# Two chained MLPs behind a chunked scan on one core: other places for the sums and remainders of the next block pair, and PSUM pools split in two

## The chip, the cores and the metric

One core of a Trainium2 chip runs the whole program in one launch. The metric is device time in microseconds (us); lower is better. The engines that matter here are TensorE (PE, matrix products), VectorE (DVE), ScalarE (ACT), GpSimd (POOL) and SyncE (SP, which issues most transfers).

## The reference

Three stages follow each other, all in float32.

```python
# 1. scan over x (4, 8, 768, 32) in chunks of 32: y = intra-chunk part + inter-chunk state part
# 2. first MLP on 3072 tokens of 256 features (d_ff 2048)
h = x @ w_in
g = np.where(h > 0.0, h, np.exp(np.minimum(h, 0.0)) - 1.0)
x = g @ w_out
# 3. second, gated MLP (d_ff 1536)
g = x @ w_gate
silu = g * (1.0 / (1.0 + np.exp(-g)))
val = x @ w_val
return (silu * val @ w_out).astype(np.float32)
```

## The kernel before, in words

**Layout.** The 3072 tokens are six blocks of 512 (`BLOCKS`). Features lie on the partitions, so a block is two tiles of 128x512, `x2[b][:, 0]` and `x2[b][:, 1]`. A float32 product is made of three TensorE products on a high part and a remainder: high x high, low x high, high x low (`mm3`, L548). The high part is a copy into the type float32r on ACT, the remainder a subtraction on DVE or POOL.

**Opening.** The scan runs in 24 units of 128 tokens. The first four units (block 0) are written out by hand in `ORDER` (L57). Odd units put their products into the PSUM tiles `cb_odd` and `y_odd` (named cbo and yo in the profile), two banks each, both of the pool `ps0` (L106). After the last entry of `ORDER`, L836 gives this pool back, and L837 opens the pool `ps` in its place, with two buffers of the tag `h` and one each of `c0` and `c1`. The last readers of `cb_odd` are L443 (DVE), those of `y_odd` L541 and L477 (DVE).

**First MLP.** Its 96 steps (6 blocks x 16 slices of 128 hidden features) are the loop at L941. Step i makes the hidden tile (`m_a`: six matmuls into `h`), then ACT and DVE apply the activation (`m_e1`, `m_e1b`; L578, L583, L584), the tile is split (`m_e2`; L561 on ACT, L562 on POOL), and the output product of three steps earlier follows (`m_c`, L605). Two buffers of `h` mean that step i+2 can't begin before DVE's L584 of step i is done. The scan units of later blocks, the weights' decoding and the preparation of the second MLP are tasks in the tables `early`, `mid`, `pe` and `late`, keyed by step. `last_a` is step 79; steps 80 to 95 are the last block.

**Second MLP.** Two blocks together are a pair p (three pairs); for each of the twelve slices f of the hidden features there is a step `s_step(j)` with j = 12p + f. The gate and value columns of a slice and the two blocks of a pair form a 2x2 product, made with seven products instead of eight. For that, each pair needs seven operands (`OPS`, L56): the four tiles b11, b21, b12/t1 and b22 and the sums t3, t1, t2, t4 (`x_sum`, L684), each with a high part (`x_hi`, L704 on ACT) and a remainder (`x_lo`, L708). They are kept in tiles `xs`; pair 1 has tiles of its own (suffix "o" in the profile) for b11, t2 and t3, and all other operands of pairs 1 and 2 overwrite those of pair 0.

A step issues on PE: 12 matmuls for the products a, b, d and c, nine more for a (b21), d (t4) and c (b22), then the 12 output matmuls `s_o` of the step before (named o, L556). Between them lie on DVE: u2 (L762, from b), u3 (L763, from d), u3 again (L770), s1 (L777), u2 again (L778), m0 (L779) and m1 (L784). On ACT: the copy of a (L758), the split of the second hidden tile of the step before (L749), the copy of c (L764), two Silu (L775, L781) and the split of the first hidden tile (L749). On POOL: the two remainders of these splits (gl, L750). The product d with t4 writes on top of what L763 has just read, so it waits for L763.

Everything else in a step is called at hooks: "a" (behind L764 in program order, ahead of L770), "b" (behind the Silu of L775, ahead of L777), "c" (behind the first split) and "d" (at the end of the step). Each engine works its instructions off in program order. The table `hooks` is filled at L904 to L920: weights of later slices (`w2_load`, `w2_hi`, `w2_sums` on POOL, `w2_lo` on DVE, all of pair 0's steps 0 to 9), and the operands of the next pair. For pair p with e = 12p the four sums are on POOL at hook "c" of steps e-5 to e-2; the high parts are at hooks "b" and "c" of steps e-3 to e-1, and their remainders on DVE at hook "d" of the same steps (t4 on POOL; b22 at hook "a" of step e).

**End of a pair.** In the second step of the next pair, `s_end` (L720) copies the four output tiles from PSUM (m = 0 on DVE, m = 1 on ACT) and issues their transfers; the last pair does so at its end (L792), where the first hidden tile's remainder is on POOL and the second's on DVE.

Of the kernel before, what the change touches and what calls it, by code (L numbers as in the profile page):

```python
# [8 lines left out]
F32 = mybir.dt.float32  # L9
F32R = mybir.dt.float32r  # L10
# [3 lines left out]
AF = mybir.ActivationFunctionType  # L14
ALU = mybir.AluOpType
PSUM = bass.MemoryType.PSUM
# [12 lines left out]
NF1, NF2 = F1 // 128, F2 // 128  # L29
# [3 lines left out]
LAG = 3  # L33
# [22 lines left out]
OPS = ["b11", "t2", "t3", "t1", "b21", "t4", "b22"]  # L56
# [10 lines left out]
def ssm_mlp_glu_kernel(ctx, tc, a, bcs, xbc, w1, w2, consts, out):  # L67
    nc = tc.nc
    NB = len(BLOCKS)
# [4 lines left out]
    work = ctx.enter_context(tc.tile_pool(name="work", bufs=3))  # L74
# [6 lines left out]
    x2 = [x2_all[:, 2 * s:2 * (s + n)].rearrange("p (k q) -> p k q", k=2) for s, n in zip(starts, BLOCKS)]  # L81
# [13 lines left out]
    ph2 = {}  # L95
# [7 lines left out]
    cb_ps = psa.tile([128, 2, 512], F32, name="cb")  # L103
    y_ps = psa.tile([128, 2, 512], F32, name="y")
    first = ExitStack()
    ps0 = first.enter_context(tc.tile_pool(name="ps0", bufs=1, space=PSUM))  # L106
    cb_odd = ps0.tile([128, 2, 512], F32, name="cbo")
    y_odd = ps0.tile([128, 2, 512], F32, name="yo")
    ap_ = ats.enter_context(tc.tile_pool(name="attn", bufs=2))
    ast = ats.enter_context(tc.tile_pool(name="attn_static", bufs=1))  # L110
    sbd = [ast.tile([128, 2, 128], F32, name=f"sbd{i}") for i in range(2)]
# [436 lines left out]
    def mm3(dst, pairs, first, last, **kw):  # L548

        ops = []  # L550
        for (lh, ll), (rh, rl) in pairs:
            ops += [(lh, rh), (ll, rh)]
        for (lh, ll), (rh, rl) in pairs:
            ops.append((lh, rl))
        for i, (l, r) in enumerate(ops):
            nc.tensor.matmul(dst, lhsT=l, rhs=r, start=first and i == 0, stop=last and i == len(ops) - 1, **kw)  # L556
# [7 lines left out]

    def m_a(b, f):
        n = BLOCKS[b]
        h = hps[b, f] = ph2["ps"].tile([128, 512], F32, tag="h", name="h", bufs=2)[:, :n]
        wh, wl = W1["i", f]
        mm3(h, [((wh[:, k], wl[:, k]), (xh_t[b][:, k], xl_t[b][:, k])) for k in range(2)], True, True)

# [19 lines left out]
    def m_c(b, f):  # L590
        n = BLOCKS[b]
        if f == 0:
            cps[b] = [ph2["ps"].tile([128, 512], F32, tag=f"c{m}", name=f"c{m}")[:, :n] for m in range(2)]
        g = gt.pop((b, f))
        if b == 0:
            for m in range(2):
                nc.tensor.matmul(cps[b][m], lhsT=W1["v", f][:, m * 128:(m + 1) * 128], rhs=g, start=f == 0, stop=f == NF1 - 1)  # L597
            return
        wh, wl = W1["o", f]
        gh, gl = g  # L600
        prods = [(m, w, r) for r, ws in ((gh, (wh, wl)), (gl, (wh,))) for m in range(2) for w in ws]
        if f in (0, NF1 - 1):
            prods.sort(key=lambda z: z[0])
        for m, w, r in prods:
            nc.tensor.matmul(cps[b][m], lhsT=w[:, m * 128:(m + 1) * 128], rhs=r,  # L605
                             start=f == 0 and w is wh and r is gh, stop=f == NF1 - 1 and r is gl)
# [84 lines left out]
    def x_hi(p, nm):  # L691
        if (p, nm) not in xs:
            k = OPS.index(nm)
            if p == 1 and k < 3:
                if k < 2:
                    z = ph2["w2l" if k else "w2h"].tile([128, WS], F32R, tag="v2", name=f"x_{nm}o")
                else:
                    z = ph2["w2h"].tile([128, 1024], F32R, name=f"x_{nm}o")
                xs[p, nm] = z[:, :512], z[:, 512:1024]
            elif p == 0:  # L700
                xs[p, nm] = [ph2["xs"].tile([128, 512], F32R, name=f"x_{nm}{z}") for z in "hl"]
            else:
                xs[p, nm] = xs[0, nm]
        nc.scalar.activation(xs[p, nm][0], XT[p][nm], AF.Copy)  # L704
# [5 lines left out]
    def s_half(j, i):  # L710
        return (ident8.rearrange("p h q -> p (h q)"))[:, 512 * i:512 * i + 512]

    def s_o(j, i, m):
        p, f = divmod(j, NF2)
        if f == 0:
            ops_[p, i, m] = ph2["ps"].tile([128, 512], F32, tag="h" if i else f"c{m}", name=f"o{i}{m}", bufs=2 if i else None)
        ms = slice(384 + m * 128, 384 + m * 128 + 128)
        mm3(ops_[p, i, m], [([w[:, ms] for w in W2[f]], gt[j, i])], f == 0, f == NF2 - 1)

    def s_end(p, i, m):  # L720
        b = 2 * p + i
        y = x2[b - 1][:, m] if i else ph2["w2h"].tile([128, 512], F32, tag="yo", name="yo", bufs=2)
        if m == 0:
            nc.vector.tensor_copy(y, ops_.pop((p, i, m)))
        else:
            nc.scalar.activation(y, ops_.pop((p, i, m)), AF.Copy)
        nc.sync.dma_start(out[m * 128:(m + 1) * 128, starts[b]:starts[b] + 512], y)

    def s_step(j, hooks):
        p, f = divmod(j, NF2)  # L730

        def hook(nm):
            for fn, args in hooks.get((j, nm), []):
                fn(*args)

        ps = {k: ph2["psv"].tile([128, 512], F32, tag=f"p{k}", name=f"p{k}") for k in "abcd"}

        def prod(k, w, nm, first):
            ws = slice(128 * w, 128 * w + 128)
            (wh, wl), (xh, xl) = [z[:, ws] for z in W2[f]], xs[p, nm]  # L740
            for i, (l, r) in enumerate(((wh, xh), (wl, xh), (wh, xl))):
                nc.tensor.matmul(ps[k], lhsT=l, rhs=r, start=first and i == 0, stop=i == 2, skip_group_check=True)  # L742

        def mtile(nm):
            return work.tile([128, 512], F32, tag="m", name=nm)

        def g_split(j, i, m, eng):
            hi, lo = [work.tile([128, 512], F32R, tag=f"g{z}", name=f"g{z}", bufs=LAG + 1) for z in "hl"]
            nc.scalar.activation(hi, m, AF.Copy)  # L749
            eng.tensor_tensor(lo, m, hi.bitcast(F32), ALU.subtract)  # L750
            gt[j, i] = hi, lo

        prod("a", 0, "b11", True)
        prod("b", 7, "t2", True)
        prod("d", 5, "t3", True)
        prod("c", 6, "t1", True)
        s1 = mtile("s1")
        nc.scalar.activation(s1, ps["a"], AF.Copy)  # L758
        if j:
            g_split(j - 1, 1, V.pop(j - 1), nc.gpsimd)  # L760
        u2, u3, s5 = s_half(j, 0), s_half(j, 1), x2[2 * max(p - 1, 0) + 1][:, 1]
        nc.vector.tensor_tensor(u2, s1, ps["b"], ALU.add)  # L762
        nc.vector.tensor_tensor(u3, u2, ps["d"], ALU.add)  # L763
        nc.scalar.activation(s5, ps["c"], AF.Copy)  # L764
        hook("a")
        if f == 1 and p:
            for i in range(2):
                for m in range(2):
                    s_end(p - 1, i, m)
        nc.vector.tensor_tensor(u3, u3, s5, ALU.add)  # L770
        prod("a", 1, "b21", False)
        prod("d", 2, "t4", False)
        prod("c", 8, "b22", False)
        m0 = mtile("m0")
        nc.scalar.activation(m0, ps["a"], AF.Silu)  # L775
        hook("b")
        nc.vector.tensor_tensor(s1, u2, ps["d"], ALU.add)  # L777
        nc.vector.tensor_tensor(u2, u2, ps["c"], ALU.add)  # L778
        nc.vector.tensor_tensor(m0, m0, s1, ALU.mult)  # L779
        m1 = mtile("m1")  # L780
        nc.scalar.activation(m1, u2, AF.Silu)  # L781
        g_split(j, 0, m0, nc.gpsimd)
        hook("c")
        nc.vector.tensor_tensor(m1, m1, u3, ALU.mult)  # L784
        V[j] = m1
        hook("o")
        if j:
            for i in range(2):
                for m in range(2):
                    s_o(j - 1, i, m)  # L790
                gt.pop((j - 1, i))
        if j == 3 * NF2 - 1:  # L792
            g_split(j, 1, V.pop(j), nc.vector)
            for i in range(2):
                for m in range(2):
                    s_o(j, i, m)
                    s_end(p, i, m)
        hook("d")


# [1 line left out]
    with tc.manual_schedule():  # L802
# [31 lines left out]
        for z in ORDER:  # L834
            tok[z]()
        first.close()  # L836
        ph2["ps"] = ctx.enter_context(tc.tile_pool(name="ps", bufs=1, space=PSUM))  # L837

        early, mid, pe, late = {}, {}, {}, {}
        late[8] = [(lambda: nc.scalar.activation(ident8, ident.unsqueeze(1).to_broadcast([128, H, Q]), AF.Copy), ())]  # L840
# [1 line left out]
        def at(when, slot, fn, *args):  # L842
            when.setdefault(slot, []).append((fn, args))
# [61 lines left out]
        for f in range(NHL, NF2):  # L905
# [4 lines left out]
            at(hooks, (f - 2, "b"), w2_hi, f, 1)  # L910
            at(hooks, (f - 2, "b"), w2_lo, f, 0)
            at(hooks, (f - 2, "d"), w2_lo, f, 1)
        for p in range(1, NB // 2):
            e = p * NF2
            for k, nm in enumerate(("t3", "t1", "t2", "t4")):
                at(hooks, (e - 5 + k, "c"), x_sum, p, nm, nc.gpsimd)
            for k, nm in enumerate(OPS):
                i, h, l = [(e - 3, "b", "d"), (e - 2, "b", "d"), (e - 2, "c", "d"), (e - 1, "b", "d"), (e - 1, "b", "d"), (e - 1, "c", "d"), (e - 1, "c", "a")][k]
                at(hooks, (i, h), x_hi, p, nm)
                at(hooks, (i + (l == "a"), l), x_lo, p, nm, nc.gpsimd if nm == "t4" else nc.vector)  # L920

        seq1 = [(b, f) for b in range(NB) for f in range(NF1)]
        def go(tasks):
# [96 lines left out]
```

## Time and profile before

| what | us |
|---|---|
| median of 3 runs | 621.52 |
| lowest and highest run | 617.13 and 621.55 |
| profiled execution, its own time | 621.05 |
| its span, first to last instruction | 619.3 |
| PE, DVE, ACT, POOL busy in it | 596.2, 468.5, 369.6, 365.0 |

The profiled execution's own time is 1.75 us longer than its span. The opening takes up to 23.9 us, the first MLP from there to 329.4, the second MLP from there to the end. "Busy" counts instructions in flight on an engine; matmuls are pipelined, so that one of 0.39 us starts every 0.23 us.

### The profile page before, as it was taken

How to read it: one execution, taken by the hardware profiler on the slowest of the kernel's cores; microseconds unless marked ns; L12 is line 12 of the kernel's file. 1: busy time of each engine (PE TensorE's matmuls, PEld its weight loads, DVE VectorE, ACT ScalarE, POOL GpSimd, SP SyncE). 2: the span in 40 equal slices, each digit the busy share in tenths (PEclk: the TensorE clock that was granted, in tenths of full speed). 3: DMA queues.
4: the chain of work that ended last, by engine and by line, in shares of the span. 5: the costliest groups of instructions: out<-in, count | busy, mean ns of one | idle time of the engine just before them, and what ended most of it. 6: DMA issues, size and time to landing. Idle time of an engine off the chain costs nothing.

```text
span 619.3 us, 9832 instructions
## 1 busy us (share of the span) xinstructions
PE 596.2 (96%) x3524; PEld 469.7 (76%) x3524; DVE 468.5 (76%) x676; ACT 369.6 (60%) x659; POOL 365.0 (59%) x326
## 2 busy tenths in 40 slices
PE   6899999999999999999999999978999998999997
PEld 4556667888888888778878777866888886888885
DVE  6898866768878789795644999899666679766664
ACT  1456657776668667776876555545544455544443
POOL 4444559997887887774765666756333456333332
PEclk9999999999999999999999999999999999999999
DMA  7698533345466666622010011100100000100001
GB/s 210 214 287 244 180 100 113 111 138 174 164 178 207 203 200 205 212 78 78 25 52 23 29 52 52 52 1 0 69 1 1 1 0 1 69 1 1 1 0 68
DMA packets 22744, 58.70 MB, mean 95 GB/s; under 512 B 3736, under 2 KB 6168, under 8 KB 22696
## 3 DMA queue, kind: packets, MB, share of 16 engines
q1 hardware_dynamic: 20664, 53.18, 27.6%
q10 hardware_dynamic: 2032, 4.90, 2.1%
q8 instruction: 27, 0.44, 0.3%
q14 instruction: 21, 0.17, 0.1%
HBM read 50.12 MB, written 7.96 MB: 94 GB/s over the span
## 4 chain that ended last, share of the span: by engine, by line
PE 62%; issue 10%; DVE 6%; POOL 5%; DMA 4%; ACT 1%; POOLq 0%; DVEq 0%; ACTq 0%
PE h L556 16%; PE c L605 15%; PE o L556 10%; PE pd L742 5%; POOL gl L750 5%; PE pa L742 5%; PE pc L742 4%; DMA w2e<-in_w 4%; PE pb L742 3%; PE cb L432 1%; PE y L509 1%; PE c L597 1%; DVE w2l L670 1%; DVE ident L763 1%; DVE ident L762 1%
## 5 line engine op out<-in xcount | busy, mean ns | idle before, releaser
L750 POOL TENSOR_TENSOR gl<-m,gh 128x512 fp32r<-128x512 f32 x71 | 94.6, 1333 | 133.6 <-ACT gh L749 133.6
L562 POOL TENSOR_TENSOR gl<-m,gh 128x512 fp32r<-128x512 f32 x80 | 110.6, 1383 | 43.5 <-ACT gh L561 42.1
L584 DVE SCALAR_TENSOR_TENSOR m<-m,h 128x512 f32<-128x512 f32 x96 | 65.5, 683 | 55.1 <-ACT m L583 53.2
L578 ACT ACTIVATE m<-h 128x512 f32<-128x512 f32 x96 | 56.8, 592 | 48.4 <-PE h L556 42.4
L556 PE MATMUL h<-xh,wih 128*128 128x512 f32 x192 | 81.3, 424 | 2.9 <-DVE x L477 1.9
L556 PE MATMUL h<-xh,wil 128*128 128x512 f32 x192 | 76.1, 396 | 0.0
L605 PE MATMUL c<-gh,woh 128*128 128x512 f32 x160 | 62.4, 390 | 0.0
L605 PE MATMUL c<-gh,wol 128*128 128x512 f32 x160 | 62.3, 389 | 0.0
L583 ACT ACTIVATE m<-m 128x512 f32<-128x512 f32 x96 | 59.8, 623 | 0.5
L556 PE MATMUL h<-xl,wih 128*128 128x512 f32 x192 | 59.8, 393 | 0.0
L781 ACT ACTIVATE m<-ident 128x512 f32<-128x512 f32 x36 | 22.8, 633 | 61.4 <-DVE ident L778 61.4
L556 PE MATMUL o<-gl,w2h 128*128 128x512 f32 x144 | 56.2, 390 | 0.4 <-POOL gl L750 0.4
L556 PE MATMUL o<-gh,w2h 128*128 128x512 f32 x144 | 56.2, 390 | 0.0
L556 PE MATMUL o<-gh,w2l 128*128 128x512 f32 x144 | 56.1, 390 | 0.0
L762 DVE TENSOR_TENSOR ident<-s,pb 128x512 f32<-128x512 f32 x36 | 24.6, 683 | 40.4 <-PE pb L742 36.6
L561 ACT ACTIVATE gh<-m 128x512 fp32r<-128x512 f32 x80 | 50.1, 626 | 6.0 <-DVE m L584 5.8
L605 PE MATMUL c<-gl,woh 128*128 128x512 f32 x160 | 50.9, 389 | 0.0
L556 PEld LDWEIGHTS h<-xh,wih 128*128 128x128 f32 x192 | 36.6, 190 | 15.4 <-DVE m L584 3.5
L393 POOL TENSOR_TENSOR xb<-xb,P 128x128 f32<-128x128 f32 x16 | 38.0, 2374 | 14.2 <-DVE P L387 14.2
L749 ACT ACTIVATE gh<-m 128x512 fp32r<-128x512 f32 x72 | 45.2, 628 | 1.2 <-DVE m L779 1.0
L764 ACT ACTIVATE x<-pc 128x512 f32<-128x512 f32 x36 | 21.5, 598 | 35.3 <-PE pc L742 35.3
L556 PEld LDWEIGHTS h<-xl,wih 128*128 128x128 f32 x192 | 36.5, 190 | 8.0
(226 smaller groups left out, 1470.9 us busy)
## 6 DMA issues: line engine op xcount, KB each, us to landing
w2e<-in_w SPq DMA_DIRECT2D x12, 768.0 KB
abc<-ac SPq DMA_DIRECT2D x16, 512.0 KB
bcraw<-in_bcs SPq DMA_DIRECT2D x32, 256.0 KB
w2e<-in_w SPq DMA_DIRECT2D x14, 512.0 KB
xb<-in_xbc SPq DMA_DIRECT2D x18, 256.0 KB
v2d<-w2e ACTq DMA_DIRECT2D x12, 384.0 KB
v<-v2d SPq DMA_DIRECT2D x12, 384.0 KB
out_y<-yo SPq DMA_DIRECT2D x6, 256.0 KB
```

The lines of the kernel that those rows point to most:

```text
L393: nc.gpsimd.tensor_tensor(u["ct"], u["ct"], u["P"], ALU.mult)
L556: nc.tensor.matmul(dst, lhsT=l, rhs=r, start=first and i == 0, stop=last and i == len(ops) - 1, **kw)
L561: nc.scalar.activation(hi, src, AF.Copy)
L562: lo_eng.tensor_tensor(lo, src, hi.bitcast(F32), ALU.subtract)
L578: nc.scalar.activation(m, h, AF.Relu, scale=-1.0)
L583: nc.scalar.activation(m, m, AF.Exp, scale=-1.0)
L584: nc.vector.scalar_tensor_tensor(m, m, -1.0, h, ALU.add, ALU.max)
L605: nc.tensor.matmul(cps[b][m], lhsT=w[:, m * 128:(m + 1) * 128], rhs=r, start=f == 0 and w is wh and r is gh, stop=f == NF1 - 1 and r is gl)
L742: nc.tensor.matmul(ps[k], lhsT=l, rhs=r, start=first and i == 0, stop=i == 2, skip_group_check=True)
L749: nc.scalar.activation(hi, m, AF.Copy)
L750: eng.tensor_tensor(lo, m, hi.bitcast(F32), ALU.subtract)
L762: nc.vector.tensor_tensor(u2, s1, ps["b"], ALU.add)
```

## The change

The PSUM tiles `cb_odd` and `y_odd` lie in two pools, and so do the tags `h` and `c0`/`c1` that take their place. The operand t1 of pair 1 has tiles of its own, in the place of the two buffers `yo`; the outputs are copied into `x2` tiles of a later pair instead. The four sums of pair 1 are on DVE in steps 88 to 91 of the first MLP, those of pair 2 on DVE at hook "b" of steps 15 to 18. High parts and remainders are together at one hook: for pair 1, t3 at "d" of step 0, b11 and t2 at "b" of step 10, t1 at "a" of step 11; for pair 2, b11, t2, t3, t1 at "b" of steps 18 to 21; b21 at "b" of step e-1, with the high parts of t4 and b22 behind it, t4's remainder on POOL at "d" of e-1, and b22's on DVE at "a" of step e. At the end of the last step, the first hidden tile's remainder is on DVE, the last output matmuls are in another order, and the last output tile is copied in two halves on DVE and ACT.

```diff
-    ps0 = first.enter_context(tc.tile_pool(name="ps0", bufs=1, space=PSUM))
-    cb_odd = ps0.tile([128, 2, 512], F32, name="cbo")
-    y_odd = ps0.tile([128, 2, 512], F32, name="yo")
+    cb_odd = first.enter_context(tc.tile_pool(name="ps0", bufs=1, space=PSUM)).tile([128, 2, 512], F32, name="cbo")
+    y_odd = first.enter_context(tc.tile_pool(name="ps1", bufs=1, space=PSUM)).tile([128, 2, 512], F32, name="yo")
...
-            if p == 1 and k < 3:
+            if p == 1 and k < 4:
...
-    def s_end(p, i, m):
+    def s_end(p, i, m, cut=False):
         b = 2 * p + i
-        y = x2[b - 1][:, m] if i else ph2["w2h"].tile([128, 512], F32, tag="yo", name="yo", bufs=2)
-        if m == 0:
-            nc.vector.tensor_copy(y, ops_.pop((p, i, m)))
+        y, o = x2[min(2 * p + 2, NB - 2) + i][:, m], ops_.pop((p, i, m))
+        if cut:
+            nc.vector.tensor_copy(y[:, :256], o[:, :256])
+            nc.scalar.activation(y[:, 256:], o[:, 256:], AF.Copy)
+        elif m == 0:
+            nc.vector.tensor_copy(y, o)
...
-        g_split(j, 0, m0, nc.gpsimd)
+        end = j == NB // 2 * NF2 - 1
+        g_split(j, 0, m0, None if end else nc.gpsimd)
...
-        if j == 3 * NF2 - 1:
+        if end:
+            nc.vector.tensor_tensor(gt[j, 0][1], m0, gt[j, 0][0].bitcast(F32), ALU.subtract)
             g_split(j, 1, V.pop(j), nc.vector)
-            for i in range(2):
+            for k in range(2):
                 for m in range(2):
-                    s_o(j, i, m)
-                    s_end(p, i, m)
+                    s_o(j, 0, m, (slice(0, 2), slice(2, 3))[k])
+            for m in range(2):
+                s_end(p, 0, m)
+            for m in range(2):
+                s_o(j, 1, m)
+                s_end(p, 1, m, m)
...
-        ph2["ps"] = ctx.enter_context(tc.tile_pool(name="ps", bufs=1, space=PSUM))
+        ph2["h"] = ctx.enter_context(tc.tile_pool(name="ps", bufs=1, space=PSUM))
+        ph2["c"] = ctx.enter_context(tc.tile_pool(name="psc", bufs=1, space=PSUM))
...
-        for p in range(1, NB // 2):
+        for k, nm in enumerate(("t3", "t1", "t2", "t4")):
+            at(late, last_a + 9 + k, x_sum, 1, nm, nc.vector)
+            at(hooks, (NF2 + 3 + k, "b"), x_sum, 2, nm, nc.vector)
+        for p, where in ((1, dict(t3=(0, "d"), t1=(11, "a"), b11=(10, "b"), t2=(10, "b"))), (2, dict(b11=(18, "b"), t2=(19, "b"), t3=(20, "b"), t1=(21, "b")))):
             e = p * NF2
-            for k, nm in enumerate(("t3", "t1", "t2", "t4")):
-                at(hooks, (e - 5 + k, "c"), x_sum, p, nm, nc.gpsimd)
-            for k, nm in enumerate(OPS):
-                i, h, l = [(e - 3, "b", "d"), (e - 2, "b", "d"), (e - 2, "c", "d"), (e - 1, "b", "d"), (e - 1, "b", "d"), (e - 1, "c", "d"), (e - 1, "c", "a")][k]
-                at(hooks, (i, h), x_hi, p, nm)
-                at(hooks, (i + (l == "a"), l), x_lo, p, nm, nc.gpsimd if nm == "t4" else nc.vector)
+            for nm, z in where.items():
+                at(hooks, z, x_hi, p, nm)
+                at(hooks, z, x_lo, p, nm, nc.vector)
+            at(hooks, (e - 1, "b"), x_hi, p, "b21")
+            at(hooks, (e - 1, "b"), x_lo, p, "b21", nc.vector)
+            at(hooks, (e - 1, "b"), x_hi, p, "t4")
+            at(hooks, (e - 1, "b"), x_hi, p, "b22")
+            at(hooks, (e - 1, "d"), x_lo, p, "t4", nc.gpsimd)
+            at(hooks, (e, "a"), x_lo, p, "b22", nc.vector)
```

## Rows read from the trace of the kernel before

**Rows 1.** The page's busy time by engine, whole span.

```profile
PE 596.2 (96%) x3524; PEld 469.7 (76%) x3524; DVE 468.5 (76%) x676; ACT 369.6 (60%) x659; POOL 365.0 (59%) x326
```

**Rows 2.** PE's waits: for whom, us in total, times, longest.

```profile
PE pd L742 <- DVE ident L763: 7.8, 8, 2.2
...
PE h L556 <- DVE x L477: 1.9, 1, 1.9
```

**Rows 3.** Chain that ended last: the output matmuls of steps 8, 13 and 14.

```profile
397.86 2.72 PE o L556 x12
...
442.09 2.72 PE o L556 x12
449.57 2.72 PE o L556 x12
```

**Rows 4.** PE in order of time: one stall of step 10; starts of steps 23, 25.

```profile
415.06 0.50 PE L742 MATMUL pd<-x_t4h,w2h 128*128 128x512 f32 x1 [2.16 <-DVE ident L763]
...
511.97 0.39 PE L742 MATMUL pa<-x_b11o,w2h 128*128 128x512 f32 x1
...
529.70 0.39 PE L742 MATMUL pa<-x_b11h,w2h 128*128 128x512 f32 x1
```

**Rows 5.** DVE in order of time, in step 17 and into step 18.

```profile
471.37 0.69 DVE L777 TENSOR_TENSOR s<-ident,pd 128x512 f32<-128x512 f32 x1
...
473.61 0.69 DVE L784 TENSOR_TENSOR m<-m,ident 128x512 f32<-128x512 f32 x1 [0.15 <-ACT m L781]
476.18 0.69 DVE L762 TENSOR_TENSOR ident<-s,pb 128x512 f32<-128x512 f32 x1 [1.88 <-PE pb L742]
```

**Rows 6.** ACT in order of time, the same stretch.

```profile
470.75 0.60 ACT L775 ACTIVATE m<-pa 128x512 f32<-128x512 f32 x1
...
473.49 0.63 ACT L749 ACTIVATE gh<-m 128x512 fp32r<-128x512 f32 x1
475.45 0.60 ACT L758 ACTIVATE s<-pa 128x512 f32<-128x512 f32 x1 [1.33 <-PE pa L742]
```

**Rows 7.** POOL in order of time, the same stretch.

```profile
474.20 1.28 POOL L750 TENSOR_TENSOR gl<-m,gh 128x512 fp32r<-128x512 f32 x1 [3.74 <-ACT gh L749]
```

**Rows 8.** DVE in order of time: remainders at the end of step 10 and in step 12.

```profile
418.92 1.82 DVE L708 TENSOR_TENSOR x_t2o<-x,x_t2o 128x512 fp32r<-128x512 f32 x1
...
432.58 0.69 DVE L708 TENSOR_TENSOR x_b22l<-x,x_b22h 128x512 fp32r<-128x512 f32 x1
```

**Rows 9.** POOL in order of time, end of step 10.

```profile
418.90 1.29 POOL L750 TENSOR_TENSOR gl<-m,gh 128x512 fp32r<-128x512 f32 x1 [4.14 <-ACT gh L749]
```

**Rows 10.** ACT in order of time, start of step 1.

```profile
339.14 0.60 ACT L758 ACTIVATE s<-pa 128x512 f32<-128x512 f32 x1
```

**Rows 11.** DVE in order of time, step 92 of the first MLP.

```profile
321.94 0.69 DVE L584 SCALAR_TENSOR_TENSOR m<-m,h 128x512 f32<-128x512 f32 x1 [0.42 <-ACT m L583]
```

**Rows 12.** POOL in order of time, step 91 of the first MLP.

```profile
321.46 1.29 POOL L562 TENSOR_TENSOR gl<-m,gh 128x512 fp32r<-128x512 f32 x1 [0.49 <-PE c L605]
```

**Rows 13.** PE in order of time: step 94's first matmul.

```profile
323.98 0.39 PE L556 MATMUL h<-xh,wih 128*128 128x512 f32 x1
```

**Rows 14.** PE in order of time: the first MLP's first matmul.

```profile
23.91 0.77 PE L556 MATMUL h<-xh,wih 128*128 128x512 f32 x1 [1.86 <-DVE x L477]
```

**Rows 15.** PE's groups from 24 to 28 us: count, busy us, mean ns, idle.

```profile
L556 PE MATMUL h<-xh,wil 128*128 128x512 f32 x4 | 2.4, 603 | 0.0
```

**Rows 16.** DVE in order of time: the last reader of cbo.

```profile
17.70 0.68 DVE L443 TENSOR_TENSOR w2e<-w2e,cbo 128x512 f32<-128x512 f32 x1
```

**Rows 17.** ACT in order of time: unit 3's high part.

```profile
22.16 0.38 ACT L537 ACTIVATE xh<-yo 128x256 fp32r<-128x256 f32 x1 [1.05 <-PE yo L521]
```

**Rows 18.** All engines in order of time, the end.

```profile
611.61 1.29 POOL L750 TENSOR_TENSOR gl<-m,gh 128x512 fp32r<-128x512 f32 x1 [3.74 <-ACT gh L749]
...
612.95 0.50 PE L556 MATMUL o<-gl,w2h 128*128 128x512 f32 x1 [0.35 <-POOL gl L750]
...
615.54 0.60 ACT L726 ACTIVATE x<-o 128x512 f32<-128x512 f32 x1 [0.77 <-PE o L556]
```

More of the change, by code (lines that the diff above doesn't have):

```diff
@@ L566, in m_a @@
         n = BLOCKS[b]
-        h = hps[b, f] = ph2["ps"].tile([128, 512], F32, tag="h", name="h", bufs=2)[:, :n]
+        h = hps[b, f] = ph2["h"].tile([128, 512], F32, tag="h", name="h", bufs=2)[:, :n]
         wh, wl = W1["i", f]
@@ L592, in m_c @@
         if f == 0:
-            cps[b] = [ph2["ps"].tile([128, 512], F32, tag=f"c{m}", name=f"c{m}")[:, :n] for m in range(2)]
+            cps[b] = [ph2["c"].tile([128, 512], F32, tag=f"c{m}", name=f"c{m}")[:, :n] for m in range(2)]
         g = gt.pop((b, f))
@@ L711, in s_half, with s_o @@
         return (ident8.rearrange("p h q -> p (h q)"))[:, 512 * i:512 * i + 512]
-    def s_o(j, i, m):
+    def s_o(j, i, m, part=slice(0, 3)):
         p, f = divmod(j, NF2)
-        if f == 0:
-            ops_[p, i, m] = ph2["ps"].tile([128, 512], F32, tag="h" if i else f"c{m}", name=f"o{i}{m}", bufs=2 if i else None)
+        if (p, i, m) not in ops_:
+            ops_[p, i, m] = ph2["h" if i else "c"].tile([128, 512], F32, tag="h" if i else f"c{m}", name=f"o{i}{m}", bufs=2 if i else None)
         ms = slice(384 + m * 128, 384 + m * 128 + 128)
-        mm3(ops_[p, i, m], [([w[:, ms] for w in W2[f]], gt[j, i])], f == 0, f == NF2 - 1)
-    def s_end(p, i, m):
+        (wh, wl), (gh, gl) = [w[:, ms] for w in W2[f]], gt[j, i]
+        for k, (l, r) in list(enumerate(((wh, gh), (wl, gh), (wh, gl))))[part]:
+            nc.tensor.matmul(ops_[p, i, m], lhsT=l, rhs=r, start=f == 0 and k == 0, stop=f == NF2 - 1 and k == 2)
+    def s_end(p, i, m, cut=False):
         b = 2 * p + i
-        y = x2[b - 1][:, m] if i else ph2["w2h"].tile([128, 512], F32, tag="yo", name="yo", bufs=2)
-        if m == 0:
-            nc.vector.tensor_copy(y, ops_.pop((p, i, m)))
+        y, o = x2[min(2 * p + 2, NB - 2) + i][:, m], ops_.pop((p, i, m))
[4 more added lines that the diff above has]
+            nc.vector.tensor_copy(y, o)
         else:
-            nc.scalar.activation(y, ops_.pop((p, i, m)), AF.Copy)
+            nc.scalar.activation(y, o, AF.Copy)
         nc.sync.dma_start(out[m * 128:(m + 1) * 128, starts[b]:starts[b] + 512], y)
@@ L747, in g_split @@
         def g_split(j, i, m, eng):
-            hi, lo = [work.tile([128, 512], F32R, tag=f"g{z}", name=f"g{z}", bufs=LAG + 1) for z in "hl"]
+            hi, lo = gt[j, i] = [work.tile([128, 512], F32R, tag=f"g{z}", name=f"g{z}", bufs=LAG + 1) for z in "hl"]
             nc.scalar.activation(hi, m, AF.Copy)
-            eng.tensor_tensor(lo, m, hi.bitcast(F32), ALU.subtract)
-            gt[j, i] = hi, lo
+            if eng is not None:
+                eng.tensor_tensor(lo, m, hi.bitcast(F32), ALU.subtract)
         prod("a", 0, "b11", True)
```

## Prediction, made before the changed kernel ran

> **What bounds the kernel now.** I read the page's busy shares first: PE works 596.2 of 619.3 us [rows 1], so time can come only from PE's idle places and from slow restarts behind them. PE's waits come next. Past the opening the large one is the matmul `pd` of t4 waiting for DVE's L763, 7.8 us in eight stalls; the opening has one wait of 1.9 us on L477 [rows 2]. The chain that ended last then tells what these stalls cost in whole steps. From the output matmuls of step 13 to those of step 14 it takes 449.57 - 442.09 = 7.48 us: a step without a stall. From step 8 to step 13 it takes 442.09 - 397.86 = 44.23 us for five steps, 5 x 7.48 = 37.40, so the entry into pair 1 loses 6.83 us [rows 3]. The entry into pair 2 loses 529.70 - 511.97 - 2 x 7.48 = 2.77 us in steps 23 and 24 [rows 4]. These losses are larger than the listed idle times, because PE restarts slowly after each stall.
>
> Why DVE is late shows in one undisturbed step. DVE ends m1 at 473.61 + 0.69 = 474.30 and idles 1.88 us until the next u2 at 476.18 [rows 5]. What is put at the end of a step (hook "d") has these 1.88 us. A remainder alone takes 0.69 us, but the one at 418.92 takes 1.82 [rows 8], because POOL's gl started 0.02 us before it and ran until 420.19 [rows 9]. Steps 10 and 11 have two such remainders at "d" (step 9 has three lots of work there), about 3.6 us in 1.88. So u2, u3 and then `pd` come late, up to the 2.16 us stall of step 10 [rows 4].
>
> **The change part by part.**
>
> *Entry into pair 1.* The remainders leave hook "d" and meet DVE at "b", ahead of s1. There POOL is idle: its gl of 474.20 had 3.74 us of idle time before it, from 470.46 [rows 7], and s1 starts at 471.37 [rows 5]. So a remainder costs 0.69 there, not 1.82. But its high part stands just before it: it starts on ACT when Silu of m0 ends, 470.75 + 0.60 = 471.35 [rows 6], takes 0.63 (I take the L749 row for it, same shape) and ends at 471.98; the remainder ends at about 472.7, and s1 comes 1.33 us late. DVE's slack of 1.88 covers it. ACT's slack does too, just: its copy of a had 1.33 us of idle time behind L749 [rows 6]. So one operand at "b" costs nothing. Step 10 has two: the second adds 0.69, 2.0 in all, so the next u2 is some 0.15 late on DVE and some 0.7 on ACT's side, less small overlaps; I take 0.2 for step 11. In step 11, t1 at "a" and b21 at "b" hold DVE for about 2.0 us again: 0.2 for step 12. Step 12 has b22 at "a" beside POOL's remainder of t4: 0.2 for step 13. Steps 9 and 10 keep the weights' remainder at "d" of the step before, one alone, which ends 1.82 us after m1, about where u2 is due: 0.15 each. Together 0.9 in place of 6.83, so -5.9. Bounds: nothing left (-6.8), or half of it left because ACT's queue holds the high parts back (-3.4).
>
> *POOL.* Its four sums at "c" of steps 7 to 10 and 19 to 22 go. Each took a turn between the two gl and so blocked L770 on DVE; this is part of the 6.83 and 2.77 and isn't counted again.
>
> *Entry into pair 2.* Steps 15 to 17 have one sum at "b", 0.69 us without an ACT step before it: covered. Step 18 has a sum, which runs while ACT makes the high part, and then one remainder; steps 19 to 21 and 23 have one. All are the covered case. 0.1 stays of 2.77: -2.7. Bounds: -2.8, and -1.2 if every one of these five steps runs over by 0.3.
>
> *Step 0.* The new operand t3 of pair 1 at "d" puts one conversion on ACT ahead of the copy of a in step 1, which today starts at 339.14 with no idle time before it [rows 10]. The copy comes 0.63 later, u2 with it; a part goes into the lateness that step 2 has already. +0.15, between 0 and +0.6.
>
> *Sums of pair 1 in the first MLP's last block.* Four DVE operations of 0.69 us in steps 88 to 91. Step 92's L584 starts at 321.94 after 0.42 us idle and ends at 322.63 [rows 11]; step 94, which needs its buffer, starts at 323.98 [rows 13]: 1.35 us of slack. The sum of t4 falls right before it and meets POOL's gl, 321.46 to 322.75 [rows 12]. If DVE waits for POOL there, as the remainder beside gl did [rows 8, 9], the sum ends at about 323.4 and L584 at 324.1, 0.1 past the need; if it gets in ahead, it costs nothing: +0.2, between 0 and +0.6. The Trainium skill (SBUF — State Buffer, "SBUF: two separate sides") speaks against this move: the port pair that the two engines share is locked for a whole instruction by whichever starts first. By it the sum waits; [rows 8, 9] agree with their 1.82 in place of 0.69 us.
>
> *Opening.* The first hidden tile waits for L477, the last reader of `y_odd`, 1.86 us [rows 14]. In a pool of its own it waits for L443, done at 18.38 [rows 16]; next late is the high part of unit 3, done at 22.54 [rows 17]. So PE can start at about 22.65 in place of 23.91: 1.25 us. Not all of it need last: the matmuls from 24 to 28 us take 603 ns each [rows 15] against 390 later [rows 4], PE's lower level, 1.2 of 2.4 GHz, and what is done earlier at that level counts half, 0.6 us, if the rise to full speed doesn't come earlier too. I take -0.8, between 0 (no effect) and -1.86 (the whole wait). The Trainium skill (TensorE: Matmul & The Clock Gate, "What's actually happening") speaks against a rise that moves along: activity is judged in windows that run free of the program's start. By it the gain may be 0.6 us, otherwise 1.25.
>
> *The PSUM pools later.* `s_o` takes its tiles from the same four banks as before; `s_end` copies as before into other tiles, whose readers are done by step 12 or 24. Nothing.
>
> *End.* Today the matmul of 612.95 waits 0.35 us for a POOL remainder that starts at 611.61 and takes 1.29 [rows 18]. On DVE, free after m1, it takes 0.69, and the four matmuls with high parts go first: PE saves the 0.35 and the restart, about 0.6. The last copy, 0.60 on ACT, is halved over two engines: 0.15. -0.75, between -0.4 and -0.9.
>
> **Sum.** -5.9 - 2.7 + 0.15 + 0.2 - 0.8 - 0.75 = -9.8. The profiled execution took 621.05 us, so 611.25, say 611.3. It stands 0.5 below the median of 621.52; one run was 617.13, 4.4 lower, so runs scatter by up to that. All good bounds give -12.4, 608.7; all bad ones -3.8, 617.3.
>
> **Rivals.**
>
> 1. *ACT becomes late.* High parts at "b" go ahead of the second Silu and of L749, and ACT's 1.33 us of slack [rows 6] is as small as the delay. If each operand there overran by 0.5, with the restart 0.8, over eight steps, 4 to 6 us of the gain would go: 614 to 617. For it: the delay and the slack are equal. Against: `pd` needs u3, not u2, and ACT starts an instruction shortly before the last one ends.
>
> 2. *Slower: hook "b" isn't free of POOL.* If sums and remainders at "b" took 1.82 as in [rows 8], s1 would come 2.5 late, beyond both slacks, and steps 10 to 12, 18 to 21 and 23 would lose 1.1 each, steps 15 to 17 (no high part) 0.5 each, and step 10's second operand 1.8: 8.8 + 1.5 + 1.8 = 12.1 in place of 9.6, no gain in the opening and +0.35 before it, so 621.05 + 2.5 + 0.35 - 0.4 = 623.5. It decides from an overrun of about 0.9 per step. Against: POOL's 3.74 us of idle time just there [rows 7].
>
> 3. *A hidden wait.* t3's new tile lies in memory that the first MLP gives back at the end of step 0, and the outputs now sit where later sums are written. If a transfer or a release held ACT for several us, the gain would shrink to less than 1%: 616 to 621. Against: the readers are done by then, and the sums come two steps after the outputs.
>
> 4. *More than counted*: both entries without loss and the whole opening wait, 608.7, and less by the scatter of runs: 606 to 609.
>
> **How the numbers follow.** A measurement of this kernel tells about 1% from no change, here 6.2 us: 615.3. Forecast (609 to 614) 0.68, rival 1 0.17, rival 2 0.03, rival 3 0.06, rival 4 0.06. Faster by over 1%: 0.68 + 0.06 + 0.12 of rival 1 = 0.86; within 1%: 0.05 + 0.06 + 0.01 of rival 2 = 0.12; slower: 0.02. The range 607.0 to 615.0 takes in the forecast, most of rival 4 and the near part of rival 1.
>
> **What would show it right or wrong.** Right: `pd` waits for L763 under 2 us in total, steps 9 to 13 within 1 us of 5 x 7.48, steps 23 and 24 at 7.48, every L708 on DVE near 0.69, the first L556 near 22.65, no PE wait on POOL at the end. Wrong: L708 still at 1.8, ACT without idle time before L758 in steps 18 to 21, or PE waiting at 324 us.

## The result, and the profile after

The changed kernel takes 610.73 us in the median of 4 runs (610.05 to 612.17), the kernel before 621.29 beside it; the ratio is 0.9849, with a 95% interval of 0.9803 to 0.9894. A later repetition, beside other runs of the kernel before, gave 610.65 us and 0.9838 (0.9826 to 0.9851). The forecast was 611.3. The profiled execution took 610.05 us, its span is 608.3. One run of the last experiment below took 1450.32 us, and its ratio leaves that run out.

Where the 11.0 us between the two spans come from, by the start of each step's first `pa` matmul in the time order of PE (steps counted over the second MLP). Below, a step "loses" what it takes above the 7.48 us of a step without a stall.

| stretch | before, us | after, us | difference | forecast |
|---|---|---|---|---|
| start to step 0 (opening, first MLP) | 329.42 | 327.93 | -1.49 | -0.6 |
| steps 0 to 8 | 71.00 | 70.96 | -0.04 | +0.15 |
| steps 9 to 13 (entry into pair 1) | 44.23 | 37.80 | -6.43 | -5.9 |
| steps 14 to 22 | 67.32 | 67.32 | 0 | 0 |
| steps 23, 24 (entry into pair 2) | 17.73 | 14.96 | -2.77 | -2.7 |
| steps 25 to 34 | 74.80 | 74.80 | 0 | 0 |
| step 35 to the end | 14.77 | 14.50 | -0.27 | -0.75 |

Not all of this repeats. In the profile of the repetition steps 0 to 8 take 71.07 us and steps 9 to 13 38.13, mostly because step 10 loses 0.33 there; the rows below are the same. The first row scatters by more than its difference (last section).

The page's busy times of the changed kernel:

```profile
PE 594.0 (98%) x3524; PEld 469.6 (77%) x3524; DVE 461.9 (76%) x686; ACT 369.1 (61%) x659; POOL 351.1 (58%) x317
```

PE does the same 3524 matmuls as in [rows 1] in a span that is 11.0 us shorter; POOL loses nine instructions and DVE gains ten. PE's waits (for whom, us in total, times, longest):

```profile
PE h L555 <- DVE m L583: 1.3, 2, 0.9
...
PE h L555 <- ACT xh L536: 0.5, 1, 0.5
...
PE pd L746 <- DVE ident L767: 0.4, 2, 0.3
```

The wait of `pd` was 7.8 us in [rows 2] and is 0.4; the opening's wait for L477 is gone, and a shorter one for unit 3's high part stands there. One wait has grown, that of `h` for the activation's last operation; the longest of its kind is 0.9 us. The chain that ended last shows whole steps, as in [rows 3]:

```profile
396.31 2.74 PE o L719 x12
...
434.13 2.72 PE o L719 x12
441.61 2.72 PE o L719 x12
```

From step 8 to step 13 it now takes 37.82 us, 0.42 above five free steps of 7.48. What DVE does in steps 10 to 12, in order of time:

```profile
411.18 0.69 DVE L707 TENSOR_TENSOR x_b11o<-x,x_b11o 128x512 fp32r<-128x512 f32 x1 [0.51 <-ACT x_b11o L703]
411.79 0.68 DVE L707 TENSOR_TENSOR x_t2o<-x,x_t2o 128x512 fp32r<-128x512 f32 x1
...
417.98 0.69 DVE L707 TENSOR_TENSOR x_t1o<-x,x_t1o 128x512 fp32r<-128x512 f32 x1 [0.85 <-ACT x_t1o L703]
...
419.19 0.68 DVE L707 TENSOR_TENSOR x_b21l<-x,x_b21h 128x512 fp32r<-128x512 f32 x1
...
424.44 1.26 DVE L707 TENSOR_TENSOR x_b22l<-x,x_b22h 128x512 fp32r<-128x512 f32 x1
```

The remainders that took 1.82 us at hook "d" [rows 8] take 0.68 at "a" and "b", and the 0.51 and 0.85 us of idle time before two of them are the waits for ACT's high part. Only b22, beside POOL's remainder of t4, still takes 1.26. ACT has become nearly as tight as feared, without harm (ACT in order of time, end of step 11 and start of step 19):

```profile
421.36 0.63 ACT L785 ACTIVATE m<-ident 128x512 f32<-128x512 f32 x1 [1.36 <-DVE ident L782]
421.90 0.63 ACT L753 ACTIVATE gh<-m 128x512 fp32r<-128x512 f32 x1
422.44 0.58 ACT L762 ACTIVATE s<-pa 128x512 f32<-128x512 f32 x1
...
474.97 0.60 ACT L762 ACTIVATE s<-pa 128x512 f32<-128x512 f32 x1 [0.19 <-PE pa L746]
```

The copy of a (L762) had 1.33 us of idle time before it in [rows 6]. At 422.44 it has none, but step 12 still loses only 0.10 us; in steps 19 to 22, with one operand at "b" each, 0.19 to 0.20 us are left and nothing is lost.

The opening and one place of the first MLP, PE in order of time:

```profile
22.33 0.79 PE L555 MATMUL h<-xh,wih 128*128 128x512 f32 x1 [0.54 <-ACT xh L536]
...
26.34 0.63 PE L555 MATMUL h<-xh,wil 128*128 128x512 f32 x1
...
261.08 0.50 PE L555 MATMUL h<-xh,wih 128*128 128x512 f32 x1 [0.89 <-DVE m L583]
```

The first hidden tile begins 1.59 us earlier than in [rows 14]. At the third one 1.02 us of that is left, by step 72 it has grown to 1.97, and at step 73 (261.08) 0.48 is lost again. There ACT had waited for a weight load of the second MLP:

```profile
257.80 0.92 ACT L136 ACTIVATE w2e<-w2e 128x768 f32<-128x768 f32 x1 [2.69 <-DMA w2e<-in_w]
```

PE's idle time at this place was 0.41 us before the change. From step 72 to step 73 it takes 3.77 us here and 3.29 before, but 2.87 to 4.08 over the ten profiles of kernels with this opening, so the 0.48 us are scatter. The sums of pair 1 in steps 88 to 91 cost nothing: the lead is 1.50 us at step 88 and 1.49 at step 95.

The end, all engines in order of time:

```profile
603.49 0.69 DVE L728 COPY x<-o 128x512 f32<-128x512 f32 x1 [0.21 <-PE o L719]
...
603.74 0.39 PE L719 MATMUL o<-gl,w2h 128*128 128x512 f32 x1
604.17 0.42 DVE L725 COPY x<-o 128x256 f32<-128x256 f32 x1
604.63 0.38 ACT L726 ACTIVATE x<-o 128x256 f32<-128x256 f32 x1 [1.22 <-DVE x L725]
```

PE's wait of [rows 18] is gone: from the start of step 35 to the end of its last matmul it takes 10.36 us in place of 11.01. But the halves of the last tile are copied one after the other, and the last copy ends at 605.01, 0.88 us after the last matmul; before it was 0.63. The rest to the end of the span took 3.26 us in place of 3.13. In all, 0.27 us of PE's 0.65 reach the end of the span. What the DMA engines do meanwhile (stretch, its length, busy time of PE, PEld, DVE, ACT and POOL, clock, DMA share, GB/s):

```profile
604.50:605.50 1.00, 0.00 (x0) 0.00 (x0) 0.09 (x1) 0.38 (x1) 0.00 (x0) 1.00 1.04 399
605.50:606.50 1.00, 0.00 (x0) 0.00 (x0) 0.00 (x0) 0.00 (x0) 0.00 (x0) 1.00 1.07 412
```

They are full (a share can pass 1, since a packet counts where it starts) with the four transfers of the output tiles, until 606.88, and the span ends 1.4 us after that, as long after the last packet as before the change. So the last copy, done at 605.01, isn't what the end waits for. The first of the four transfers is issued 9.53 us into step 35 (603.30), 0.18 earlier than before (9.71, at 614.21), although PE is 0.65 earlier at its end.

### The profile page after: what moved, and what is told of

It is laid out like the page before. It is cut to its first block, busy times and chain, and to the rows that moved or that the text cites. A ratio compares the mean times of both kernels' runs of the same rounds, so it can differ in the third digit from the quotient of the medians.

```text
span 608.3 us, 9830 instructions
## 1 busy us (share of the span) xinstructions
PE 594.0 (98%) x3524; PEld 469.6 (77%) x3524; DVE 461.9 (76%) x686; ACT 369.1 (61%) x659; POOL 351.1 (58%) x317
## 4 chain that ended last, share of the span: by engine, by line
PE 91%; DVE 3%; DMA 3%; ACT 1%; issue 1%; SPq 0%; POOL 0%; ACTq 0%; DVEq 0%; POOLq 0%
PE h L555 21%; PE o L719 16%; PE c L604 16%; PE pd L746 8%; PE pc L746 8%; PE pa L746 8%; PE c L596 5%; PE pb L746 4%; DMA w2e<-in_w 2%; PE cb L431 1%; PE y L508 1%; PE y L504 1%; PE cb L436 1%; DMA abc<-in_a 0%; PE y L453 0%
## 5 line engine op out<-in xcount | busy, mean ns | idle before, releaser
L555 PE MATMUL h<-xh,wih 128*128 128x512 f32 x192 | 81.6, 425 | 1.8 <-DVE m L583 1.3
L555 PE MATMUL h<-xh,wil 128*128 128x512 f32 x192 | 76.1, 396 | 0.0
L555 PE MATMUL h<-xl,wih 128*128 128x512 f32 x192 | 60.1, 395 | 0.0
L766 DVE TENSOR_TENSOR ident<-s,pb 128x512 f32<-128x512 f32 x36 | 24.7, 685 | 35.1 <-PE pb L746 31.9
L555 PEld LDWEIGHTS h<-xh,wih 128*128 128x128 f32 x192 | 36.5, 190 | 13.9 <-DVE m L583 2.6
L555 PEld LDWEIGHTS h<-xl,wih 128*128 128x128 f32 x192 | 36.6, 191 | 8.1
L555 PEld LDWEIGHTS h<-xh,wil 128*128 128x128 f32 x192 | 36.7, 191 | 7.9 <-issue 1.4
```

## The experiments

The first three test what carried the entries into the pairs and whether the halved copy spoilt the end, the next three what is still lost in steps 1 to 9, then come the PSUM pools, then two of the versions together.

**Sums of pair 2 back on POOL.** The remainders stay at "b", but can't come before the sums, so they move by one to three steps.

```diff
-            at(hooks, (NF2 + 3 + k, "b"), x_sum, 2, nm, nc.vector)
+            at(hooks, (2 * NF2 - 5 + k, "c"), x_sum, 2, nm, nc.gpsimd)
...
-        for p, where in (..., (2, dict(b11=(18, "b"), t2=(19, "b"), t3=(20, "b"), t1=(21, "b")))):
+        for p, where in (..., (2, dict(b11=(20, "b"), t3=(21, "b"), t1=(22, "b"), t2=(22, "b")))):
```

> The four sums of pair 2 go back to POOL at hook c of steps 19 to 22, the remainders stay at hook b (steps 20 to 23). Theory A (the place of the remainders is what counts: at b POOL is idle, at d its gl holds DVE up): steps 19 to 24 lose at most 0.5 us in all, remainders on DVE take about 0.7 us. Rival (the sums on POOL delay gl and block DVE's L774-type additions, and that was the loss): steps 19 to 24 lose 2 to 2.8 us, as before the change.

Steps 23 and 24 lose 0.49 and 0.20 us, steps 19 to 22 nothing: 0.69, a little above theory A's 0.5 and far from the rival's 2. In step 22, the hardest one, POOL and DVE read so (in order of time, first POOL):

```profile
500.38 1.30 POOL L688 TENSOR_TENSOR x<-x 128x512 f32<-128x512 f32 x1
501.64 1.30 POOL L755 TENSOR_TENSOR gl<-m,gh 128x512 fp32r<-128x512 f32 x1
```

```profile
501.78 1.71 DVE L774 TENSOR_TENSOR ident<-ident,x 128x512 f32<-128x512 f32 x1 [0.51 <-ACT x L768]
503.41 0.68 DVE L707 TENSOR_TENSOR x_t1l<-x,x_t1h 128x512 fp32r<-128x512 f32 x1
504.01 0.68 DVE L707 TENSOR_TENSOR x_t2l<-x,x_t2h 128x512 fp32r<-128x512 f32 x1
```

The sum pushes gl back by its own length, gl now holds up the addition L774 (1.71 in place of 0.69 us), but the two remainders behind it are free.

**Remainders of pair 2 back at "d".** The sums stay on DVE in steps 15 to 18; pair 2 gets the old table of hooks for its high parts and remainders.

```diff
-        for p, where in (..., (2, dict(b11=(18, "b"), t2=(19, "b"), t3=(20, "b"), t1=(21, "b")))):
+        for p, where in (...,):
...
+        e = 2 * NF2
+        for k, nm in enumerate(OPS):
+            i, h, l = [(e - 3, "b", "d"), (e - 2, "b", "d"), (e - 2, "c", "d"), (e - 1, "b", "d"), (e - 1, "b", "d"), (e - 1, "c", "d"), (e - 1, "c", "a")][k]
+            at(hooks, (i, h), x_hi, 2, nm)
+            at(hooks, (i + (l == "a"), l), x_lo, 2, nm, nc.gpsimd if nm == "t4" else nc.vector)
```

> The sums of pair 2 stay on DVE at hook b of steps 15 to 18, but its high parts and remainders go back to the places of before (remainders at hook d of steps 21 to 23). Theory A: remainders take 1.8 us again and steps 23 and 24 lose 2.4 to 2.8 us together, so about 612.7 us. Rival (the sums on POOL were the loss): under 0.5 us lost.

Steps 23 and 24 lose 0.24 and 1.38 us, 1.62 together, between the two theories. DVE in order of time, ends of steps 22 and 23:

```profile
503.57 1.82 DVE L707 TENSOR_TENSOR x_t2l<-x,x_t2h 128x512 fp32r<-128x512 f32 x1
505.32 0.68 DVE L707 TENSOR_TENSOR x_t3l<-x,x_t3h 128x512 fp32r<-128x512 f32 x1
...
511.29 1.82 DVE L707 TENSOR_TENSOR x_t1l<-x,x_t1h 128x512 fp32r<-128x512 f32 x1
513.03 1.78 DVE L707 TENSOR_TENSOR x_b21l<-x,x_b21h 128x512 fp32r<-128x512 f32 x1
```

The first remainder at "d" waits for gl in both steps. The second is free in step 22, where no sum follows gl on POOL; in step 23 POOL still has t4's remainder there (512.52, 1.75 us), and the second one waits too. So the sums were a part of the loss of their own. Of pair 2's 2.77 us, moving the sums alone saves 1.15, moving the remainders alone 2.08, both 2.77; 0.46 is in either. For pair 1 this split was not tried.

**The last tile copied whole.**

```diff
-                s_end(p, 1, m, m)
+                s_end(p, 1, m)
```

> The last output tile is copied whole by ACT, not in halves. Theory A (the two halves run one after the other, 0.42 and 0.38 us, so halving made the end longer): from the end of the last matmul to the end of the last copy 0.63 us in place of 0.88, so 0.25 us less from there to the end of the span. Rival (the halves save time, and the later end comes from the DVE copy ahead of them): the same 0.88 us or more.

0.63 us from the last matmul's end to the last copy's end: so far theory A. But its second half, 0.25 us less to the end of the span, doesn't come: the rest of the way is 3.51 us here and 3.26 in the changed kernel, and from the start of step 35 to the end of the span both take 14.50. That isn't chance: it is 14.50 or 14.51 in all eight profiles with the halves and 14.50 in all three without (this one and the two of the last experiment). The end waits for the transfers, and the halving neither saves nor costs. The single time, 608.65 us, is low because step 0 starts 1.41 us earlier (326.52), by scatter of the opening (below).

**The weights' second remainder from "d" to "a" of the next step.**

```diff
-                at(hooks, (f - 4, "d"), w2_load, f)
+                at(hooks, (f - 3, "a"), w2_load, f)
...
-            at(hooks, (f - 2, "d"), w2_lo, f, 1)
+            at(hooks, (f - 1, "a"), w2_lo, f, 1)
```

> The weights' second remainder of pair 0 goes from hook d of step f-2 to hook a of step f-1, and the load into the freed tile behind it. Theory A (what is still lost in steps 1 to 8, 2.28 us, is the same wait of a DVE remainder at d on POOL's gl): steps 1 to 9 lose under 1 us, about 608.5 us. Rival (DVE is full in these steps, with two remainders and POOL's weight sums beside its seven operations, wherever they stand): 2 us or more stay lost, 610 us or later, or more because the load and the weight sums come later.

Steps 1 to 9 lose 3.62 us, more than the 2.28 of the changed kernel, and step 10 another 0.49; 612.53 us. The load comes later, so POOL's sums of the weights begin with the next step and push both gl together in front of the moved remainder (step 7, POOL, then DVE):

```profile
383.74 0.46 POOL L654 TENSOR_TENSOR v<-v 128x128 f32<-128x128 f32 x1 [1.86 <-DMA v<-v2d]
...
386.44 2.54 POOL L755 TENSOR_TENSOR gl<-m,gh 128x512 fp32r<-128x512 f32 x2
```

```profile
387.87 1.67 DVE L669 TENSOR_TENSOR w2l<-v,w2h 128x512 fp32r<-128x512 f32 x1
```

The time is the rival's, but its reason isn't shown: the remainder found POOL at work at "a" as well (0.70 to 1.67 us in steps 2 to 10).

**The same remainder from "d" to "b" of the same step.**

```diff
-            at(hooks, (f - 2, "d"), w2_lo, f, 1)
+            at(hooks, (f - 2, "b"), w2_lo, f, 1)
```

> The weights' second remainder of pair 0 goes from hook d to hook b of the same step, behind the first one. Theory A (loss in steps 1 to 8 comes from the remainder that waits for gl at d): steps 1 to 9 lose under 1 us in place of 2.28. Rival B (the tile is freed earlier, so the next load and POOL's weight sums come earlier, into the middle of the next step, and block DVE there): 1.5 to 3 us lost, DVE operations in mid-step above 0.9 us.

1.78 us lost in steps 1 to 9, rival B's range. The weight sums on POOL now fall beside L774 and the two remainders (in step 6 the sums at 381.03, 382.02 and 382.90 take 0.91 to 0.92 us each in place of 0.46, L774 takes 1.00, the remainders 1.08 and 0.94).

**POOL's work taken away instead.** In steps 1 to 9 the first hidden tile's remainder is on DVE, behind m1.

```diff
-        g_split(j, 0, m0, None if end else nc.gpsimd)
+        g_split(j, 0, m0, None if end or 0 < j < 10 else nc.gpsimd)
...
         V[j] = m1
+        if 0 < j < 10:
+            nc.vector.tensor_tensor(gt[j, 0][1], m0, gt[j, 0][0].bitcast(F32), ALU.subtract)
```

> In steps 1 to 9 the first hidden tile's remainder is made on DVE right behind m1, not on POOL, so that nothing of POOL runs at the step's end beside the weights' remainder; loads and sums stay where they are. Theory A: both remainders take 0.7 us, 1.4 in the 1.88 us that DVE has, steps 1 to 9 lose under 0.6 us in place of 2.28. Rival (DVE is simply full in these steps): 2 us or more lost, since DVE now has one more operation per step.

Steps 1 to 9 lose 0.53 us: theory A. DVE in order of time at the end of step 7:

```profile
389.52 0.71 DVE L789 TENSOR_TENSOR m<-m,ident 128x512 f32<-128x512 f32 x1 [0.16 <-ACT m L785]
390.15 0.68 DVE L792 TENSOR_TENSOR gl<-m,gh 128x512 fp32r<-128x512 f32 x1
390.76 0.68 DVE L669 TENSOR_TENSOR w2l<-v,w2h 128x512 fp32r<-128x512 f32 x1
391.42 0.69 DVE L766 TENSOR_TENSOR ident<-s,pb 128x512 f32<-128x512 f32 x1
```

DVE has one operation more per step and is in time. It wasn't full: it was waiting for POOL.

**The PSUM pools joined again**, in the changed kernel:

```diff
+    ps0 = first.enter_context(tc.tile_pool(name="ps0", bufs=1, space=PSUM))
-    cb_odd = first.enter_context(tc.tile_pool(name="ps0", bufs=1, space=PSUM)).tile([128, 2, 512], F32, name="cbo")
-    y_odd = first.enter_context(tc.tile_pool(name="ps1", bufs=1, space=PSUM)).tile([128, 2, 512], F32, name="yo")
+    cb_odd = ps0.tile([128, 2, 512], F32, name="cbo")
+    y_odd = ps0.tile([128, 2, 512], F32, name="yo")
...
-        ph2["c"] = ctx.enter_context(tc.tile_pool(name="psc", bufs=1, space=PSUM))
+        ph2["c"] = ph2["h"]
```

> The changed kernel with its PSUM pools joined again as before. Theory A (the split lets the first MLP begin earlier and that lasts): first hidden matmul at 23.6 to 24.0 us in place of 22.2 to 23.0, waiting for the last reader of yo, and a median 1 to 1.6 us above the changed kernel's 610.73. Rival (what PE does before its clock rises counts half, and the rise comes when it comes): the same first matmul, but under 0.7 us above it.

The wait for L477 is back (PE in order of time):

```profile
24.09 0.76 PE L556 MATMUL h<-xh,wih 128*128 128x512 f32 x1 [1.85 <-DVE x L477]
```

The first hidden matmul starts at 24.09, in place of 22.19 to 23.04 in the ten profiles with split pools: this part of theory A is shown. The median of four runs is 612.14 us (611.05 to 612.77), 1.4 above the changed kernel's 610.73, theory A's size. But the two weren't measured beside each other, single runs of the two overlap, and the ratios, each to its own runs of the kernel before, are 0.9845 (0.9799 to 0.9890) and 0.9849. So the times alone don't show what the split is worth. The profiles lean to theory A: step 0 starts at 329.83 here and at 329.42 in the kernel before, and at 328.10 on average over the ten with split pools; but three of the ten start it at 329.05 or later.

**Two versions together**: the last tile whole, and the first hidden tile's remainder on DVE in steps 1 to 9, tried twice; the second time beside the changed kernel itself.

> The changed kernel with the last output tile copied whole by ACT and the first hidden tile's remainder on DVE in steps 1 to 9. If both theories hold, 0.25 us less at the end and 1.7 us less in steps 1 to 9: about 608.8 us in the median. If neither holds, 610.7 us or more.

> The changed kernel once more, beside the next run, to compare the two on one chip. About 610.7 us in the median, runs between 609.5 and 612.5.

> The changed kernel with the last tile copied whole and the first hidden tile's remainder on DVE in steps 1 to 9, beside the run before. If both gains are real, its median lies 1.5 to 2.2 us below that of the changed kernel (0.25 at the end, 1.7 in steps 1 to 9). If the scatter of the opening (2.7 us among profiled runs with the same code up to there) hides it, less than 1 us.

The first time 608.91 us (607.76 to 612.74), ratio 0.9808 (0.9743 to 0.9872). The second time 608.38 us in the median of six and 0.9804 (0.9791 to 0.9816), beside 610.65 us and 0.9838 (0.9826 to 0.9851) of the changed kernel. The intervals are apart, and the medians differ by 2.27 us, a little more than the 1.5 to 2.2 forecast. The parts differ from the forecast's: in the second pair's profiles step 0 starts within 0.1 us (327.93 and 328.01), steps 1 to 9 lose 0.47 and 2.39 us, steps 10 to 13 0.16 and 0.73, and from step 35 to the end both take 14.50 us. So all of the gain is the remainder's, none the whole copy's.

## Why the prediction was right, and where its terms were off

*What bounds.* Right: PE's idle places in the second MLP were `pd` waiting for a late DVE, and DVE was late because its operations with two inputs in SBUF waited for POOL. The runs show this from both sides: remainders moved off POOL's busy time fall from 1.82 to 0.68 us, POOL moved away from the remainders (the run with gl on DVE) does the same, and remainders put beside other POOL work (at "a", or "b" with the weight sums there) rise again, to 1.67 or near 1. What doesn't wait fits too: DVE's L766, with one input in PSUM, takes 0.68 us at 393.13 while POOL's gl runs from 393.02 to 394.37, and over all 36 steps it takes 0.67 to 0.69. The Trainium skill (SBUF — State Buffer, "SBUF: two separate sides") describes the wait as a lock held for a whole instruction; the trace agrees: in [rows 8, 9] the remainder ends 0.55 us after gl.

*Entry into pair 1.* -5.9 forecast, -6.43 measured, within the bounds. The steps 11 to 13 were put at 0.2 each and lost 0.08, 0.10, 0.22; steps 9 and 10 at 0.15 each and lost nothing, because there DVE's remainder at "d" went ahead of gl. That was luck: in the repetition's profile it waited before step 10, which lost 0.33, and the entry gained 6.10. One reading was wrong without consequence: hook "d" of step 9 had two remainders on DVE (410.11 and 411.85), not three lots of work.

*Entry into pair 2.* -2.7 forecast, -2.77 measured. The step "this is part of the 6.83 and 2.77 and isn't counted again" was right for the sum, but it hid that moving POOL's sums saves 1.15 of the 2.77 us by itself. The place of the remainders saves 2.08 by itself, so it is the larger part, but not all.

*Rivals.* Rival 1 (ACT) is refuted by the 0.10 us of step 12 and by steps 18 to 24, which lose nothing, though with only 0.19 us of ACT's slack left; rival 2 by the 0.68 us at "b". Rival 3 wanted 616 us or more. Two of the signs named for "right" missed: b22's remainder took 1.26 and 0.84 us in place of 0.69, since t4's remainder is beside it on POOL, and the first L555 came at 22.33.

*Step 0 and steps 1 to 8.* +0.15 forecast, -0.04 measured: step 1 lost 0.24 that it didn't lose before, step 2 lost 0.27 in place of 0.65, and the others went up or down by up to 0.5. So they do between executions of the same code: step 6 loses 0.13 to 0.62 us over the five profiles whose code is the changed kernel's up to step 14.

*Sums in the last block.* +0.2 forecast, 0.0 measured; the bound of no cost held. The sum of t4 did get in ahead: it starts at 320.28 and takes 0.68 us, POOL's gl starts at 320.31 and takes 1.81. So it is in all eleven profiles of kernels with these sums.

*Opening.* The term "I take -0.8" was too small for this pair of executions, though within its bounds: 1.59 us at the first matmul, 1.49 at step 0. With 3.4 us of scatter at step 0 one pair shows little; the average of the ten profiles lies 1.3 us below the kernel before, which leans the same way. The start at 22.65 came at 22.33, since unit 3 itself was 0.27 earlier in this execution.

The clock's step was right where it stood. The matmuls at 25.06, 25.48 and 25.91 start 0.43 us apart, those at 28.75, 28.99 and 29.23 0.24 apart: the pace of the lower level and of the upper. (The profile's clock column shows 1.00 for both stretches, because the trace's first entry on the clock, full speed, comes only at 27.88 us, and at 28.13 in the kernel before.) So the first matmul moved by 1.59 us and the rise by 0.25, and at the third hidden tile 1.02 of the 1.59 us was left. By the rule of free-running windows (the Trainium skill, TensorE: Matmul & The Clock Gate, "What's actually happening") that is as expected. It is one case of many: over the ten profiles the rise comes anywhere from 24.78 to 28.95 us. What the forecast missed is that the lead came back in the first MLP, up to step 72. Why it grew there was not tried.

*End.* Here the prediction's path was wrong. It took PE's gain and the last copy's as gains of the end; PE's part came (0.65 for 0.6), but the end hangs on the output transfers, which fill the DMA engines from 604.5 to 606.5 and started only 0.18 us earlier. So -0.27 in place of -0.75, outside the bounds of -0.4 to -0.9. The term "the last copy is halved over two engines: 0.15" is worth nothing: ACT's half waits for DVE's half, the last copy ends 0.25 us later than a whole one, and no profile shows a difference at the end of the span. Whether the halves follow each other because they write one tile or because they read one PSUM tile was not tried.

So the forecast -9.8 met -11.0 with errors of both signs: +0.5 at the end, and -0.9 and -0.5 in the opening and pair 1. That the sum came so close is in part luck, since the opening's row alone scatters by more than 1.2 us.

## What to carry to other kernels

Put DVE work with two SBUF inputs where POOL is idle, and look at what POOL does just before and beside it: in [rows 8, 9] one gl of 1.29 us made a DVE remainder of 0.69 us take 1.82. An operation that is 2.6 times as long as its twin is the sign in the profile. Where both must work at the same time, it can pay to give DVE the POOL operation too, as in steps 1 to 9 (2.28 us lost became 0.53). Before shortening the last copy, look at whether the transfers of the tiles ahead of it still fill the DMA engines; here they did, and the end didn't move.

## What the runs showed that was not expected

A few hundredths of a microsecond decide who waits. In the changed kernel's step 8 POOL's gl begins at 391.38, DVE's remainder at 391.43: DVE takes 1.79 us. One step later DVE is ahead of gl, at 398.92, and takes 0.95 (a weight sum is still on POOL until 399.31); gl follows at 399.28 and takes 1.74. Before step 10 the profile can't even tell them apart: at 406.71 DVE takes 0.68, although gl's start (406.69, 1.86 us) is listed 0.02 us earlier; in the repetition, with gl at 406.87, DVE takes 1.82 from 406.90. The losses of steps 1 to 10 jump between 0 and 0.6 us by this (DVE, in order of time, first the changed kernel):

```profile
391.43 1.79 DVE L669 TENSOR_TENSOR w2l<-v,w2h 128x512 fp32r<-128x512 f32 x1
...
398.92 0.95 DVE L669 TENSOR_TENSOR w2l<-v,w2h 128x512 fp32r<-128x512 f32 x1
...
406.71 0.68 DVE L669 TENSOR_TENSOR w2l<-v,w2h 128x512 fp32r<-128x512 f32 x1
```

Then the repetition:

```profile
406.90 1.82 DVE L669 TENSOR_TENSOR w2l<-v,w2h 128x512 fp32r<-128x512 f32 x1
```

The opening scatters by itself. In the ten profiles of kernels that have the changed kernel's code up to step 0, the first hidden matmul starts between 22.19 and 23.04 us, but step 0 starts between 326.52 and 329.89. PE's pace rises at different times: in the run with the last tile whole, the matmul at 25.64 already takes 0.39 us, where the changed kernel's at 26.34 takes 0.63. A single execution therefore says nothing about changes of 1 or 2 us here; the steps of the second MLP, read one by one, do, from about 0.5 us on.

In the run with the last tile whole, PE in order of time:

```profile
25.34 0.46 PE L555 MATMUL h<-xh,wil 128*128 128x512 f32 x1
25.64 0.39 PE L555 MATMUL h<-xh,wih 128*128 128x512 f32 x1
```
